# One start modulo 256 bytes for the tiles that matmuls read, and evacuations ahead of preparations in the spatial product

## The chip, the cores and the metric

One core of a Trainium2 chip runs the whole program as one launch. The metric is the device time of that launch in microseconds (us). The kernel before took 2926.91 us, the median of three runs (2926.86, 2926.91 and 2934.82).

## What is computed

Three layers in a row, all in float32, on x of 4 batches, 3072 tokens and 256 features:

```python
X = np.fft.fft(np.fft.fft(x, axis=1), axis=2).real          # layer 1
h = np.maximum(X @ w_in, 0.0)                                # layer 2
u, v = h[..., :512], h[..., 512:]
v_n = (v - mean(v)) / sqrt(var(v) + 1e-6)                    # over the 512 features
v_s = einsum("ts,bsd->btd", w_spatial, v_n) + b_spatial[None, :, None]
y = ((u * v_s) @ w_out).reshape(12288, 256)
out = (sigmoid(y @ w_gate) * (y @ w_val)) @ w_out2           # layer 3
```

`w_spatial` is 3072 by 3072: the product over tokens is most of the work.

## The kernel before, in words

Every product is done with both operands split into a high part (12 bits less, by a ScalarE cast to float32r) and a low part (VectorE subtracts the high part); `mm3` (L257) issues three matmuls for one product: high by high (L259), low by high (L260), high by low (L261). A matmul has a moving operand (up to 512 columns) and a stationary one (128 columns).

The program has three stages, one after the other on TensorE:

- **First stage** (to about 292 us): the transforms and `x @ w_in` with the transform of the features folded into it, in units per batch; tables `c1`, `c2`, `c3`, transformed rows `ph`/`pl`, weights `g`. It leaves v and u in DRAM and the mean and root of each token's v in `ln_of`.
- **Spatial stage** (to about 1824 us): the product with `w_spatial` by a Strassen-like scheme with 7 products (`ORDER`, `V_OF`, `W_OF`) of 2 batch pairs (p) and 3 column groups (c): 42 *leaves*, each of 6 steps (kp) of 24 matmuls of 512 columns into four PSUM banks. Two sets of four banks take turns.
- **Gate stage** (to the end): 144 groups of 33 matmuls, 7 products of `x` by `wg` and 4 of `g` by `wv` in each.

In the loop over leaves (from L1205) a step kp of leaf n issues, in this order: `advance(6n + kp + 3, 2)`, which on the SP queue issues the loads of two steps on (`load_due`, into the 7 buffers `st`), on ScalarE normalises the v tiles that are due (`norm_job`, L802), and for each due tile (`prepare_job`) adds two tiles on VectorE (L819 for w, L815 for v), casts the high part on ScalarE (L821), and issues the *previous* tile's low part on VectorE (L824, held back in `lows`); then the 24 matmuls; then, for kp under 4, `evacuate` of bank kp of the leaf before. A tile that is prepared in a step is read by matmuls three steps later (`LEAD = 3`), and `wr` holds four w tiles. Where c is 2, the v tiles of the next product are due as well, one each step, so that such a step prepares two tiles instead of one.

`evacuate` adds a bank into the sums on VectorE. In the 24 leaves whose product is in `FINAL` it also multiplies by u (L1062), casts the gate's high part `gh` on ScalarE (L1068), and issues the low part `gl` (L1070) only with the next evacuation, or in `finish_gate`. In steps 4 and 5 the same loop issues `second` after the step's matmuls: 12 matmuls that read all four `gh`, `gl`, a copy of the bank on ScalarE (L1109) and a store. `second` calls `finish_gate` itself. Each engine and the SP queue works strictly in the order of issue.

**Where tiles lie.** Tiles of a pool stand one behind another, each rounded up to 32 bytes in a partition; pools are stacked from the left side (from byte 16,512, which is 128 modulo 256) or from the right side (down from byte 229,344, which is 224 modulo 256). As the kernel before is laid out, the starts modulo 256 of what matmuls read are:

| stage | left side | right side |
|---|---|---|
| first | `sps`, `spc` 128; `c3` 160; `c2`, `c1` 224; `fh`, `fl` 0 | `wih`, `wil`, `fd` 128; `g`, `nts` 0; `ph`, `pl` 0 or 128; `nt` 192 |
| spatial | `vh`, `vl`, `wh`, `wl` 128 | `woh`, `wol`, `gh`, `gl` 0 |
| gate | `wg` 128; `x0` to `x6` 128 | `x7` and the four `tail` slots 0; `gh`, `gl`, `wv` 0 |

Of the kernel before, what the change touches and what calls it, by code (L numbers as in the profile page):

```python
# [9 lines left out]
F32 = mybir.dt.float32  # L10
F32R = mybir.dt.float32r
# [8 lines left out]
B, S, D = 4, 3072, 256  # L20
# [4 lines left out]
P = 128  # L25
H = 384
R3 = H + 2

ROW = 32
RP = -(-R3 // ROW) * ROW  # L30
NT_TOK = B * S

# [201 lines left out]
FINAL = {5: (0, 1), 4: (0, 0), 2: (1, 0), 6: (1, 1)}  # L234
# [3 lines left out]
def tile_kernel(ctx: ExitStack, tc: tile.TileContext, t: dict, out: bass.AP):  # L238
# [10 lines left out]
    def f(ap):  # L249
        return ap.bitcast(F32)  # L250
# [51 lines left out]
    def pool(stack, name, bufs, side="left", **kw):  # L302
        return stack.enter_context(tc.tile_pool(name=name, bufs=bufs, side=side, reuse_waits="tile", **kw))
# [1 line left out]

    r0, l0, f0 = ExitStack(), ExitStack(), ExitStack()
    lnp = pool(ctx, "lnp", 1, "right")
    ln_of = lnp.tile([P, B * 24, 2], F32, name="ln_of")
    shifts = {}
    keep = pool(r0, "keep", 1, "right")  # L310
    pqp = pool(r0, "pqp", 2, "right")
    cst = pool(l0, "cst", 1)
    xp = pool(l0, "xp", 1)
    fop = pool(l0, "fop", 3)
    fhp = pool(l0, "fhp", 3)
    ps0 = ExitStack()
# [6 lines left out]
    nts = [keep.tile([P, R3 if unit == 3 else H], F32R, name=f"nt{unit}") for unit in range(4)]  # L323
    masks = keep.tile([P, 16], F32, name="masks")[:, : 3 + B]
    sps = cst.tile([P, B + 1, 2, P], F32R, name="sps")
    spc = cst.tile([P, SP_N], F32R, name="spc")
    cc = {}

    def load_table(p, name, shapes):

        size = sum(int(np.prod(shape)) for shape in shapes.values())
        table = p.tile([P, 2 * size], F32R, name=name)
        nc.gpsimd.dma_start(table, t[name])
        for i in range(2):
            at = i * size
            for key, shape in shapes.items():
                n = int(np.prod(shape))
                ap = table[:, at : at + n]
                names = " ".join("abc"[: len(shape)])
                ap = ap.rearrange(f"p ({names}) -> p {names}", **dict(zip("abc", shape)))  # L340
                cc.setdefault(key, []).append(ap)
                at += n
# [94 lines left out]
    tmp = pool(s0, "tmp", 1, "right")  # L437
# [45 lines left out]
    xs = tmp.tile([P, B + 1, 2, P], F32, name="xs")  # L483
    nc.sync.dma_start(xs, t["xs"])

    fn = tmp.tile([P, 2 * ROW], F32, name="fn")[:, : 12 * B].rearrange("p (s k) -> p s k", s=4)
    folds(nc.gpsimd, [(0, xn, fn)])
    load_table(cst, "c3", {"c3p": (3, R3), "c3q": (3, H)})
    nc.gpsimd.dma_start(spc, t["spc"])
    fold0(2, 0)  # L490
    fold0(2, 1)
# [2 lines left out]
    rest = convert([0, 1])  # L494
# [51 lines left out]
    rest = convert([2, 3])  # L546
# [11 lines left out]

    fold0(1, 0)
    rest()  # L560
    load_table(cst, "c2", {"c2p": (3, H), "c2q": (3, H)})
    take = first_weights(0)
    sums = [fft(fold, 0, 3, q, tiles=(2, 0), end=False, early=True) for q in range(2)]
    fold0(1, 1)
# [5 lines left out]
    take()  # L570
    spread(1)
    pq = [take_fft(*sums[q], q) for q in range(2)]
    load_table(cst, "c1", {"c1": (2, 3, H)})
    mirror_samples(slice(1, B))

    def take_nyquist(ps, n, unit):
# [8 lines left out]
    stp = pool(r0, "stp", 2, "right")  # L585
# [6 lines left out]
    def own_samples(b, unit):  # L592

        nt = stp.tile([P, RP], F32R, tag="nt", name="nt", bufs=1)[:, : R3 if unit == 3 else H]
        nc.scalar.activation(nt, f(nts[unit]), AF.Identity, scale=masks[:, 3 + b : 4 + b])
        nt_of[b, unit] = nt

    def unit_blocks(pq, b, unit):
# [5 lines left out]
        nt = nt_of.pop((b, unit))  # L604
        nb = 7 if unit == 3 else 6
        tiles = {}
        stats = stp.tile([P, 7, 6], F32, name="stats")
        mv = stp.tile([P, 7, 2], F32, name="mv")
        ve, sd = (stp.tile([P, 7], F32, name=n) for n in ("ve", "sd"))
        yp = lnb[:, unit % 2, :]  # L610


# [75 lines left out]
        def ln2():  # L688

            stt = nc.vector.scalar_tensor_tensor  # L690
            nc.vector.reciprocal(yp[:, a], sd[:, a])

            stt(out=ve[:, a], in0=yp[:, a], scalar=-0.5, in1=ve[:, a], op0=ALU.mult, op1=ALU.mult)
            nc.vector.tensor_tensor(out=ve[:, a], in0=ve[:, a], in1=yp[:, a], op=ALU.mult)
            stt(out=yp[:, a], in0=ve[:, a], scalar=1.5, in1=yp[:, a], op0=ALU.add, op1=ALU.mult)
            at = b * 24 + unit * 6
            places = [(slice(0, 6), ln_of[:, at : at + 6, :])]
            if nb == 7:
                own = stp.tile([P, 1, 2], F32, name="own")
                places.append((slice(6, 7), own))  # L700
            for k, to in places:
                nc.vector.tensor_copy(to[:, :, 0], yp[:, k])
                stt(out=to[:, :, 1], in0=mv[:, k, 0], scalar=-1.0, in1=yp[:, k], op0=ALU.mult, op1=ALU.mult)  # L703
            if nb == 7:
                q = H - (R3 - P)
                queue.dma_start(ln_of[0:1, at + 3 : at + 4, :], own[q : q + 1, :, :])
# [25 lines left out]
    jobs = []  # L732
# [17 lines left out]
    jobs = full  # L750
    tail_v = [d for d in late_v if d >= 6 * len(leaves)]
    assert not tail_v
    staged, ready, lows = {}, {}, []
    state = {"load": 0, "prep": 0}

    def source(kind, key, block):
# [21 lines left out]
    def shift_of(p, i):  # L778

        first, second, sign = V_OF[i]  # L780
        if second is None:
            return columns(p, first)[:, :, 1]
        if (p, i) not in shifts:
            shifts[p, i] = lnp.tile([P, 12], F32, name=f"shift{p}{i}")
            nc.vector.tensor_tensor(
                out=shifts[p, i],
                in0=columns(p, second)[:, :, 1],
                in1=columns(p, first)[:, :, 1],
                op=ALU.add if sign > 0 else ALU.subtract,
            )  # L790
        return shifts[p, i]

    def norm_job(n):

        _, kind, key = jobs[n]
        if kind == "v":
            p, i, kp = key
            first, second, _ = V_OF[i]
            st, scale, shift = staged[n][-1], columns(p, second or first)[:, :, 0], shift_of(p, i)
            for k in range(2):  # L800
                at = slice(2 * kp + k, 2 * kp + k + 1)
                nc.scalar.activation(st[:, k, :], st[:, k, :], AF.Identity, scale=scale[:, at], bias=shift[:, at])  # L802
# [35 lines left out]
    def advance(step, loads):  # L838

        load_due(step + loads)  # L840
        due = state["prep"]
        while due < len(jobs) and jobs[due][0] <= step:
            norm_job(due)
            due += 1
        while state["prep"] < due:
            prepare_job(state["prep"])
            state["prep"] += 1

    def start_a():
        l0.close()  # L850
# [53 lines left out]
    step = 0  # L904
# [53 lines left out]
                transform(base + AT3[q], b + 1, 3, q, pqs[b + 1, 3], None)  # L958
    transform(NYQ, B, 0, 0, None, None)
    own_samples(*units[0])  # L960
    for (b, unit), follows in zip(units, units[1:] + [None]):
        blocks, later = unit_blocks(pqs[b, unit], b, unit)
        for block in blocks:
            put_off(step, block, follows if block is blocks[-1] else None)
            for do in plan.pop(step, []):
                do()
            for first, _ in ffts.get(step, []):
                first()
            for do in lns.pop(step, []):
                do()  # L970
            for _, take in ffts.get(step, []):
                take()
            step += 1
        for k, do in enumerate(later):
            lns.setdefault(step + LAG + k, []).append(do)
# [99 lines left out]
    def finish_gate(side):  # L1075
        if "low" in side:
            side.pop("low")()
# [41 lines left out]
    p, i, c = leaves[-1]  # L1119
# [73 lines left out]
    before = None  # L1193
# [9 lines left out]
    for n, leaf in enumerate(leaves[:-1]):  # L1203
        p, i, c = leaf
        base = 4 * (n % 2)  # L1205
        ps = [banks(base + d) for d in range(4)]
        side = {"g": []}
        for kp in range(6):
            advance(6 * n + kp + LEAD, 2)
            if kp == 4:  # L1210
                side_loads(leaf, side)
            wh, wl = ready["w", (p, i, c, kp)]
            vh, vl = ready["v", (p, i, kp)]
            for k in range(2):
                for d in range(4):
                    dsl = slice(d * P, d * P + P)
                    mm3(
                        ps[d],
                        (vh[:, k, dsl], vl[:, k, dsl]),
                        (wh[:, k, :], wl[:, k, :]),  # L1220
                        kp == 0 and k == 0,
                        kp == 5 and k == 1,
                    )
            if before is not None:
                if kp < 4:
                    evacuate(before[0], before[1][kp], kp, before[2])
                elif before[0][1] in FINAL:
                    second(before[0], kp - 4, 4 - base + kp - 2, before[2])
            if n and c < 2 and before[0][1] not in FINAL:
                background()  # L1230
        before = (leaf, ps, side)
# [3 lines left out]
    n, leaf = len(leaves) - 1, leaves[-1]  # L1235
# [51 lines left out]
    before = (leaf, ps, side)  # L1287
# [76 lines left out]
    for n in range(len(groups) + 2):  # L1364
# [39 lines left out]
        if now and j + 1 < len(pairs):  # L1404
            if fb == 0:
                next_steps = x_steps(j + 1, load_raw(j + 1))
            at = {3: 0, 4: 1, 5: 2, 6: 3, 7: 4, 8: 5, 9: 6, 11: 7}
# [26 lines left out]
```

## Time and profile before

| | |
|---|---|
| median of the runs | 2926.91 us |
| the profiled execution, its own time | 2935.72 us |
| its span, first to last instruction | 2933.9 us |
| TensorE busy, matmuls | 2855.7 us (97%), 12,550 matmuls |
| VectorE, ScalarE, GpSimd busy | 2023.8, 1424.8, 224.3 us |
| mean granted TensorE clock | 0.991 |

The profiled execution is nearer to the slowest of the three runs than to the other two. Matmuls overlap: one is recorded as 0.39 us long, and the next one starts about 0.23 us after it started. A busy share says little therefore; the distance from start to start (the *pitch*) and the idle times tell where TensorE's time goes.

### The profile page before, as it was taken

To read this page: it belongs to the slowest core of one execution; us is meant where nothing else is said; L and a number is where in the kernel's file an instruction comes from. 1 tells how busy PE (TensorE), PEld (TensorE's weight loads), DVE (VectorE), ACT (ScalarE), POOL (GpSimd) and SP (SyncE) were. 2 spreads that over 40 slices of the span, in tenths; PEclk is the share of its full clock that TensorE was granted. 3 is DMA by queue.
4 is the path that set the end of the run, shared out by engine and by line. 5 is a ranking of instruction groups with operands and counts; after the bars stand their busy time and mean duration, and the time that the engine had idled before them with its cause. 6 is when DMAs were issued, how large, how long until landed. Compare 5 with 4: busy or idle time off the path is not lost.

```text
span 2933.9 us, 34266 instructions
## 1 busy us (share of the span) xinstructions
PE 2855.7 (97%) x12550; PEld 2358.3 (80%) x12550; DVE 2023.8 (69%) x3001; ACT 1424.8 (49%) x2267; POOL 224.3 (8%) x333
## 2 busy tenths in 40 slices
PE   4999999999999999999999999999999999999999
PEld 4887787888877888878887878888888888888887
DVE  7777766787756567578666476866666666676665
ACT  4787444344334244334324333656555555555554
POOL 3883000111000001000000000000000000000000
PEclk9999999999999999999999999999999999999999
DMA  6877866787756677578776474200000000000000
GB/s 232 281 274 280 274 229 234 243 312 260 254 185 227 208 264 260 171 264 297 235 251 217 155 263 139 86 29 29 29 15 15 29 29 29 15 15 29 29 15 15
DMA packets 148180, 470.76 MB, mean 160 GB/s; under 512 B 16797, under 2 KB 18333, under 8 KB 147628
## 3 DMA queue, kind: packets, MB, share of 16 engines
q1 hardware_dynamic: 140540, 434.88, 43.5%
q0 software_dynamic: 4016, 21.11, 1.8%
q10 hardware_dynamic: 3456, 12.58, 1.1%
q8 instruction: 98, 1.61, 0.2%
q14 instruction: 70, 0.57, 0.1%
HBM read 385.94 MB, written 82.58 MB: 160 GB/s over the span
## 4 chain that ended last, share of the span: by engine, by line
PE 87%; DVE 6%; issue 3%; ACT 3%; DMA 1%; POOL 0%; ACTq 0%; DVEq 0%; POOLq 0%
PE bank L261 28%; PE bank L259 28%; PE bank L260 28%; DVE vl L824 1%; DVE st L815 1%; DVE g L1062 0%; PE psf L259 0%; ACT st L802 0%; DVE gl L1070 0%; DVE wl L824 0%; DMA st<-v_d 0%; PE psf L261 0%; PE psf L260 0%; DVE st L819 0%; PE psv L260 0%
## 5 line engine op out<-in xcount | busy, mean ns | idle before, releaser
L259 PE MATMUL bank<-wh,vh 128*128 128x512 f32 x2016 | 790.1, 392 | 6.0 <-DVE ln_of L703 6.0
L261 PE MATMUL bank<-wh,vl 128*128 128x512 f32 x2016 | 789.2, 391 | 0.0
L260 PE MATMUL bank<-wl,vh 128*128 128x512 f32 x2016 | 789.2, 391 | 0.0
L824 DVE TENSOR_TENSOR wl<-st,wh 128x1024 fp32r<-128x1024 f32 x252 | 311.6, 1237 | 394.9 <-ACT wh L821 394.5
L821 ACT CAST wh<-st 128x1024 fp32r<-128x1024 f32 x252 | 264.6, 1050 | 569.6 <-PE bank L261 386.5
L259 PEld LDWEIGHTS bank<-wh,vh 128*128 128x128 f32 x2016 | 381.5, 189 | 85.9 <-DVE ln_of L703 6.7
L260 PEld LDWEIGHTS bank<-wl,vh 128*128 128x128 f32 x2016 | 382.0, 189 | 80.1
L261 PEld LDWEIGHTS bank<-wh,vl 128*128 128x128 f32 x2016 | 381.4, 189 | 80.1
L1317 DVE TENSOR_TENSOR t<-t,bank 128x512 f32<-128x512 f32 x144 | 98.9, 687 | 247.7 <-PE bank L261 247.7
L259 PE MATMUL bank<-x,wgh 128*128 128x512 f32 x673 | 265.1, 394 | 0.4 <-ACT t L1329 0.4
L261 PE MATMUL bank<-x,wgl 128*128 128x512 f32 x673 | 264.2, 393 | 0.0
L260 PE MATMUL bank<-x,wgh 128*128 128x512 f32 x673 | 264.2, 393 | 0.0
L1338 DVE TENSOR_TENSOR gl<-s,gh 128x512 fp32r<-128x512 f32 x288 | 199.3, 692 | 57.7 <-ACT gh L1336 44.5
L259 PE MATMUL bank<-gh,wv 128*128 128x512 f32 x576 | 226.2, 393 | 0.8 <-ACT gh L1331 0.8
L261 PE MATMUL bank<-gh,wv 128*128 128x512 f32 x576 | 226.6, 393 | 0.0
L260 PE MATMUL bank<-gl,wv 128*128 128x512 f32 x576 | 225.5, 391 | 0.2 <-DVE gl L1338 0.2
L819 DVE TENSOR_TENSOR st<-st 128x1024 f32<-128x1024 f32 x180 | 219.5, 1220 | 5.9 <-DMA st<-in_wt 5.7
L1308 ACT ACTIVATE s<-s 128x512 f32<-128x512 f32 x144 | 91.0, 632 | 149.9 <-DVE s L1307 149.9
L1109 ACT COPY x<-bank 128x512 f32<-128x512 f32 x48 | 28.3, 589 | 258.9 <-PE bank L261 255.9
L259 PEld LDWEIGHTS bank<-x,wgh 128*128 128x128 f32 x673 | 126.4, 188 | 30.4 <-ACT t L1329 0.9
L260 PEld LDWEIGHTS bank<-x,wgh 128*128 128x128 f32 x673 | 127.0, 189 | 28.8
L261 PEld LDWEIGHTS bank<-x,wgl 128*128 128x128 f32 x673 | 126.3, 188 | 28.6
(237 smaller groups left out, 4586.1 us busy)
## 6 DMA issues: line engine op xcount, KB each, us to landing
st<-in_wt SPq DMA_DIRECT2D x432, 512.0 KB, 5.2
st<-v_d SPq DMA_DIRECT2D x144, 512.0 KB, 4.8
u<-u_d SPq DMA_DIRECT2D x96, 256.0 KB, 4.0
u_d<-tu SPq DMA_DIRECT2D x48, 384.0 KB, 3.8
v_d<-tv SPq DMA_DIRECT2D x69, 256.0 KB, 4.3
xt<-in_xh SPq DMA_DIRECT2D x24, 512.0 KB, 4.2
x_d<-x ACTq DMA_DIRECT2D x24, 512.0 KB, 2.9
raw<-x_d SPq DMA_DIRECT2D x24, 512.0 KB, 4.2
```

Source lines behind the costliest of these rows:

```text
L259: nc.tensor.matmul(out=ps, lhsT=w[0], rhs=x[0], start=first, stop=False, **kw)
L260: nc.tensor.matmul(out=ps, lhsT=w[0], rhs=x[1], start=False, stop=False, **kw)
L261: nc.tensor.matmul(out=ps, lhsT=w[1], rhs=x[0], start=False, stop=last, **kw)
L815: nc.vector.scalar_tensor_tensor(out=st, in0=st, scalar=scale[:, at], in1=tiles[1][:, k, :], op0=ALU.mult, op1=op)
L819: nc.vector.tensor_tensor(out=tiles[0], in0=tiles[0], in1=tiles[1], op=op)
L821: nc.scalar.copy(hl[0], tiles[0])
L824: lows.append(lambda: nc.vector.tensor_tensor(out=hl[1], in0=tiles[0], in1=f(hl[0]), op=ALU.subtract))
L1109: nc.scalar.copy(side["x2"][:, o, :], ps)
L1308: nc.scalar.activation(s1, s1, AF.Sigmoid)
L1317: nc.vector.tensor_tensor(out=g["t2"], in0=g["t2"], in1=g["b"], op=ALU.add)
L1338: nc.vector.tensor_tensor(out=l, in0=s, in1=f(h), op=ALU.subtract)
```

## The change

Three things are changed.

1. **Places.** `ROW` is 64 in place of 32, so that `ph`, `pl` and `nt` are 1,792 bytes wide instead of 1,664. `ln_of` and the shifts become slices of one tile of 1,280 bytes, where `lnp` had 1,408. Small tiles (`stats`, `mv`, `ve`, `sd`, `own`) become slices of one tile `small`; three tiles called `rest` are only padding; the tables `c1`, `c2`, `c3` are allocated ahead of `spc`.
2. **Order in a spatial step.** `evacuate` (kp under 4) or `finish_gate` (kp 4 and 5) of the leaf before is issued ahead of `advance`. `second` stays behind the matmuls.
3. **Normalisation.** A v tile with kp = 0 is normalised on ScalarE in the step before the one that prepares it (set `normed` keeps it from being done twice).

```diff
-ROW = 32
+ROW = 64
...
-    ln_of = lnp.tile([P, B * 24, 2], F32, name="ln_of")
+    ln_all = lnp.tile([P, 320], F32, name="ln_all")
+    ln_of = ln_all[:, : B * 48].rearrange("p (k two) -> p k two", two=2)
...
     xp = pool(l0, "xp", 1)
+    xp.tile([P, 32], F32, name="rest")
...
     sps = cst.tile([P, B + 1, 2, P], F32R, name="sps")
+    tables = {name: cst.tile([P, t[name].shape[1]], F32R, name=name) for name in ("c1", "c2", "c3")}
     spc = cst.tile([P, SP_N], F32R, name="spc")
...
+    tmp.tile([P, 32], F32, name="rest")
+    fn = tmp.tile([P, 64], F32, name="fn")[:, : 12 * B].rearrange("p (s k) -> p s k", s=4)
...
-        stats = stp.tile([P, 7, 6], F32, name="stats")
-        mv = stp.tile([P, 7, 2], F32, name="mv")
-        ve, sd = (stp.tile([P, 7], F32, name=n) for n in ("ve", "sd"))
+        small = stp.tile([P, 72], F32, name="small")
+        stats = small[:, 0:42].rearrange("p (i k) -> p i k", k=6)
+        mv = small[:, 42:56].rearrange("p (i k) -> p i k", k=2)
+        ve, sd = small[:, 56:63], small[:, 63:70]
...
-            shifts[p, i] = lnp.tile([P, 12], F32, name=f"shift{p}{i}")
+            at = B * 48 + 12 * len(shifts)
+            shifts[p, i] = ln_all[:, at : at + 12]
...
-        if kind == "v":
+        if kind == "v" and n not in normed:
+            normed.add(n)
...
         while state["prep"] < due:
             prepare_job(state["prep"])
             state["prep"] += 1
+        while due < len(jobs) and jobs[due][0] == step + 1:
+            if jobs[due][2][-1] == 0 and due in staged:
+                norm_job(due)
+            due += 1
...
+    stp.tile([P, 48], F32, name="rest", bufs=1)
...
         for kp in range(6):
+            if before is not None:
+                if kp < 4:
+                    evacuate(before[0], before[1][kp], kp, before[2])
+                else:
+                    finish_gate(before[2])
             advance(6 * n + kp + LEAD, 2)
...
             if before is not None:
-                if kp < 4:
-                    evacuate(before[0], before[1][kp], kp, before[2])
-                elif before[0][1] in FINAL:
+                if kp >= 4 and before[0][1] in FINAL:
                     second(before[0], kp - 4, 4 - base + kp - 2, before[2])
```

## Rows read from the trace of the kernel before

**Rows 1.** The page, parts 1 and 4: busy time by engine; chain by engine.
```profile
PE 2855.7 (97%) x12550; PEld 2358.3 (80%) x12550; DVE 2023.8 (69%) x3001; ACT 1424.8 (49%) x2267; POOL 224.3 (8%) x333
...
PE 87%; DVE 6%; issue 3%; ACT 3%; DMA 1%; POOL 0%; ACTq 0%; DVEq 0%; POOLq 0%
```

**Rows 2.** Windows of PE: stretch, length us, busy (matmuls), clock, DMA share, GB/s.
```profile
1280.00:1570.00 290.00, 290.00 (x1280) 1.00 0.75 251
1850.00:2390.00 540.00, 540.00 (x2344) 1.00 0.09 30
2390.00:2920.00 530.00, 530.00 (x2294) 1.00 0.05 19
```

**Rows 3.** PE in order of time, spatial stage: start us, length us, operation.
```profile
999.95 0.39 PE L259 MATMUL bank<-wh,vh 128*128 128x512 f32 x1
...
1010.60 0.40 PE L261 MATMUL bank<-wh,vl 128*128 128x512 f32 x1
1010.84 0.39 PE L259 MATMUL bank<-gh,woh 128*128 128x512 f32 x1
...
1013.33 0.40 PE L261 MATMUL bank<-gh,wol 128*128 128x512 f32 x1
```

**Rows 4.** PE in order of time, gate stage, one group of 33 matmuls.
```profile
2299.22 0.40 PE L259 MATMUL bank<-x,wgh 128*128 128x512 f32 x1
...
2306.86 0.40 PE L259 MATMUL bank<-x,wgh 128*128 128x512 f32 x1
```

**Rows 5.** Waits of PE, whole span: total us, times, longest us.
```profile
PE bank L260 <- DVE gl L1070: 15.1, 6, 3.3
```

**Rows 6.** PE in order of time at one such wait (last: idle before).
```profile
499.25 0.39 PE L259 MATMUL bank<-gh,woh 128*128 128x512 f32 x1
502.00 0.50 PE L260 MATMUL bank<-gl,woh 128*128 128x512 f32 x1 [2.37 <-DVE gl L1070]
...
503.53 0.63 PE L259 MATMUL bank<-wh,vh 128*128 128x512 f32 x1
503.95 0.63 PE L260 MATMUL bank<-wl,vh 128*128 128x512 f32 x1
...
506.45 0.39 PE L260 MATMUL bank<-wl,vh 128*128 128x512 f32 x1
```

**Rows 7.** Window there: us, PE, PEld, DVE, ACT, POOL, clock, DMA.
```profile
504.00:512.00 8.00, 8.00 (x32) 6.53 (x31) 6.41 (x9) 3.41 (x4) 0.00 (x0) 0.85 1.01 389
```

**Rows 8.** DVE in order of time, steps 2 to 4 of that leaf.
```profile
485.86 1.22 DVE L824 TENSOR_TENSOR wl<-st,wh 128x1024 fp32r<-128x1024 f32 x1
...
493.00 1.21 DVE L824 TENSOR_TENSOR wl<-st,wh 128x1024 fp32r<-128x1024 f32 x1
...
496.53 1.22 DVE L819 TENSOR_TENSOR st<-st 128x1024 f32<-128x1024 f32 x1
...
501.26 0.68 DVE L1070 TENSOR_TENSOR gl<-g,gh 128x512 fp32r<-128x512 f32 x1
```

**Rows 9.** DVE in order of time, at the start of that leaf.
```profile
472.06 1.46 DVE L815 SCALAR_TENSOR_TENSOR st<-st,ln_of 128x512 f32<-128x512 f32 x2 [7.25 <-ACT st L802]
```

**Rows 10.** ACT in order of time: first normalisation, last gh.
```profile
471.21 1.52 ACT L802 ACTIVATE st<-st,shift,ln_of 128x512 f32<-128x512 f32 x2 [0.42 <-ACT x L1109]
...
496.04 0.62 ACT L1068 CAST gh<-g 128x512 fp32r<-128x512 f32 x1 [1.88 <-DVE g L1062]
```

**Rows 11.** Waits of ACT, whole span, and of the SP queue, 330 to 1750.
```profile
ACT wh L821 <- PE bank L261: 386.5, 110, 4.4
...
ACT st L802 <- DMA st<-v_d: 36.3, 23, 4.0
...
SPq L1081 <- DVE g L1062: 223.0, 45, 18.8
```

**Rows 12.** PE in order of time, first stage.
```profile
160.76 0.34 PE L259 MATMUL psu<-ph,gh 128*128 128x384 f32 x1
...
162.54 0.40 PE L259 MATMUL psv<-gh,ph 128*128 128x512 f32 x1
```

More of the change, by code (lines that the diff above doesn't have):

```diff
@@ L325, in tile_kernel, with load_table @@
     sps = cst.tile([P, B + 1, 2, P], F32R, name="sps")
+    tables = {name: cst.tile([P, t[name].shape[1]], F32R, name=name) for name in ("c1", "c2", "c3")}
     spc = cst.tile([P, SP_N], F32R, name="spc")
     cc = {}
-    def load_table(p, name, shapes):
+    def load_table(name, shapes):
         size = sum(int(np.prod(shape)) for shape in shapes.values())
-        table = p.tile([P, 2 * size], F32R, name=name)
+        table = tables[name]
         nc.gpsimd.dma_start(table, t[name])
@@ L484, in tile_kernel @@
     nc.sync.dma_start(xs, t["xs"])
-    fn = tmp.tile([P, 2 * ROW], F32, name="fn")[:, : 12 * B].rearrange("p (s k) -> p s k", s=4)
+    tmp.tile([P, 32], F32, name="rest")
+    fn = tmp.tile([P, 64], F32, name="fn")[:, : 12 * B].rearrange("p (s k) -> p s k", s=4)
     folds(nc.gpsimd, [(0, xn, fn)])
-    load_table(cst, "c3", {"c3p": (3, R3), "c3q": (3, H)})
+    load_table("c3", {"c3p": (3, R3), "c3q": (3, H)})
     nc.gpsimd.dma_start(spc, t["spc"])
@@ L560, in tile_kernel @@
     rest()
-    load_table(cst, "c2", {"c2p": (3, H), "c2q": (3, H)})
+    load_table("c2", {"c2p": (3, H), "c2q": (3, H)})
     take = first_weights(0)
@@ L572, in tile_kernel @@
     pq = [take_fft(*sums[q], q) for q in range(2)]
-    load_table(cst, "c1", {"c1": (2, 3, H)})
+    load_table("c1", {"c1": (2, 3, H)})
     mirror_samples(slice(1, B))
@@ L698, in ln2 @@
             if nb == 7:
-                own = stp.tile([P, 1, 2], F32, name="own")
+                own = small[:, 70:72].rearrange("p (i k) -> p i k", k=2)
                 places.append((slice(6, 7), own))
@@ L752, in tile_kernel @@
     assert not tail_v
-    staged, ready, lows = {}, {}, []
+    staged, ready, lows, normed = {}, {}, [], set()
     state = {"load": 0, "prep": 0}
```

## The prediction

> **What bounds the kernel now.** I read the page first: TensorE is busy 97% of the span and carries 87% of the chain [rows 1]. A busy share can't show whether matmuls run as fast as they could, so the next view is the windows of TensorE, in which I divide length by count. A window also counts the 1.7 matmuls that are under way at its edge (0.39 us long, one starting every 0.23 us), so 1.7 comes off each count. That gives 290.00/1278.3 = 226.9 ns in a stretch of the spatial stage, but 540.00/2342.3 = 230.5 and 530.00/2292.3 = 231.2 ns in the gate stage, at the same full clock and with no idle time in any of the three [rows 2]. The starts say it finer: in the spatial stage 47 matmuls from 999.95 to 1010.60 take 226.6 ns each [rows 3]; a group of 33 in the gate stage takes 7.64 us, 231.5 ns each [rows 4]. All have 512 columns, the same type and the same three forms, so something that is not work costs 4 to 5 ns a matmul in the gate stage.
>
> The second loss is waiting. Leaving the start of the program and the first leaf aside, TensorE's list of waits has one entry of weight: the second matmul form of a `second` waits for `gl`, 6 times, 15.1 us [rows 5]. Each is followed by a dear stretch [rows 6]: after the wait the pitch is 0.42 to 0.43 us instead of 0.227, the 1.2 GHz level in place of 2.4, and the window there shows a granted clock of 0.85 [rows 7].
>
> **Part 1, the places.** From the sizes in the code: `lnp` shrinks from 1,408 to 1,280 bytes, so that everything on the right side moves up by 128 bytes; `keep`, `cp` and `gp` then start at 128 modulo 256, where the left side starts already. `ph`, `pl` and `nt` of 1,792 bytes are 7 times 256; `nt`, `rest` and the two `small` fill 2,560 bytes, 10 times 256; the tables behind `sps` start at 128, and `spc`, `xp` and its padding bring `fh` and `fl` to 128 (18,496 + 6,176 + 128 + 32 leave no remainder). So in the spatial and the gate stage all operands start at 128, and in the first stage all but slices of `c3` and `spc` and the last windows of `ph`.
>
> What is it worth? In the spatial stage `wh` and `vh` are both at 128, and `gh` and `wo` both at 0. Both kinds run at the low pitch: 226.6 ns from 999.95 on, and 11 matmuls from 1010.84 to 1013.33 at 226.4 ns [rows 3]. Only where the class changes is a start late: 1010.60 to 1010.84 is 0.24 us for what should be 0.227 [rows 3]; at this resolution 0.01 to 0.02 us for each change of class. In the gate stage the class changes inside every group (`x` and `wg` at 128, `x7` and `tail` at 0, `gh` and `wv` at 0), and moving and stationary operand differ in part of the products. With one class everywhere it should run as the spatial stage does: (230.5 - 226.7) x 2342 = 9.0 us and (231.2 - 226.7) x 2292 = 10.4 us, together **19.5 us**. Bounds: 0, if pitch doesn't hang on places, and 21 us with the 120 matmuls outside these windows. I take 19.5, since both classes alone show the lower pitch.
> In the spatial stage 46 `second` have two changes each: 92 x 0.01 to 0.02 = 0.9 to 1.8 us; I take **1.0**. In the first stage 10 matmuls of 384 columns take 1.78 us, 178 ns [rows 12], where 226.7 less 128 columns at 2.4 GHz would be 173.4; at 4.6 ns for each of 1,086 matmuls from 60 us on that is 5.0 us at most. TensorE waits for ScalarE and VectorE there too, which takes part of it back, so between 0 and 5; I take **1.5**. The padding, the merged small tiles and the tables' new places add no instruction. What VectorE writes into the merged tiles it writes in its own order, so I cost them at nothing; bounds are nothing and a wait of the 0.2 us kind in 16 units, 3 us.
>
> One rule speaks against this part. The Trainium skill, SBUF — State Buffer, section "Who interferes with whom", gives TensorE two independent read ports and says "PE and ACT never wait on anyone"; the section "Operand start alignment" asks an operand only to start at a multiple of its element size, and adds that this is about legality, not speed. By that, part 1 would be worth 0 instead of 22 us, which is the first rival below. The trace does not agree fully: 226.6 and 231.5 ns stand side by side at one clock.
>
> **Part 2, evacuation first.** At the wait in rows 6 VectorE is not idle but late. One step of preparing two tiles and evacuating a bank takes it 493.00 - 485.86 = 7.14 us [rows 8], while TensorE's 24 matmuls take 24 x 0.2267 = 5.44 us. This happens where c is 2 and both this leaf and the one before are followed by a `second`, six times. `gl` is issued behind the preparation of step 4, which runs from 496.53 to 501.26 [rows 8], while its input `gh` is done at 496.04 + 0.62 = 496.66 [rows 10]. Moved ahead of that preparation, `gl` starts at 496.7 instead of 501.26 and ends at 497.4. TensorE asks for it at 499.25 + 0.23 = 499.48 [rows 6]: 2.1 us to spare even with nothing else moved. More is moved: the evacuation of bank 3 itself goes ahead of step 3's preparation. So all six waits should go.
> What one costs: from 499.25 to 506.45 there are 13 pitches, 7.20 us in place of 13 x 0.2267 = 2.95, so 4.25 us, of which 2.37 is the listed wait and 1.88 the clock and the way back to it [rows 6]. Six times: 15.1 + 6 x 1.88 = **26.4 us**. Bounds: 15.1 if the clock fell anyway, 26.4 if it doesn't.
>
> What moves behind: each preparation now stands behind up to four VectorE operations of 0.68 us (2.7 us). Who waits for it? TensorE, three steps later. The spare time follows from the code and one row: ScalarE's cast of a w tile waits for TensorE 110 times, 386.5 us [rows 11], because the fourth w buffer is free only when TensorE has left the step before; so in most steps a tile is ready one cast (1.05 us) and one subtraction (1.24 us) after that, 3 x 5.44 - 2.3 = 14 us before it is read. 14 covers 2.7. Behind the moved evacuation on ScalarE stands the cast `gh`, on the SP queue the load of u; both come earlier than before, and loads of two steps on come later by the same 2.7 us. What is late next in these leaves is VectorE itself: 6 preparations of 4.7 us and 4 evacuations of 2.4 us are 38 us, against TensorE's 32.6 for the products and 5.4 for the two `second`, 38 us: just even, with 14 us of lead ahead of it.
>
> **Part 3, normalising ahead.** At the start of such a leaf VectorE stood 7.25 us [rows 9], because the first normalisation stood on ScalarE behind the bank copy of `second` (it began at 471.21, straight after it) [rows 10]. Issued in the step before, it runs ahead of that copy. This gives VectorE up to 7 us in each of 13 products; none of it is on TensorE's path by itself, so **0 us**, but it adds to the 2.1 us to spare. Queued behind the normalisation on ScalarE are the bank copy and the next `gh`. It can wait for its load, as it does 23 times now, up to 4.0 us [rows 11]; 13 x 4.0 = 52 us of ScalarE, half idle, under 14 us of lead: 0 on the path.
>
> **The sum.** 19.5 + 1.0 + 1.5 + 26.4 = 48.4 us. The profiled span of 2933.9 becomes 2885.5, and its own time of 2935.72 becomes 2887.3. The profiled execution lies 8.8 us above the median and 0.9 above the slowest of the three runs. Nothing in the sum hangs on that difference, so I take it off the median: 2926.91 - 48.4 = **2878.5 us**; with runs like the profiled one it is 2887.
>
> **Rivals.**
> *Places don't matter.* The gate stage keeps 231 ns, for a reason that only goes along with the stage (more semaphores, the change of banks). For: the spatial stage is the only witness of the lower pitch. Against: both classes there have it, and changes of class cost there too. Time 2926.91 - 26.4 = 2900.5. Chance 0.11.
> *The waits stay in another place.* VectorE needs 38 us for 38, so a late load or a cast in these leaves puts `gl` late again, or another operand. For: 7.14 against 5.44 us. Against: the 2.1 us and the 7.25 us. Time 2926.91 - 22.0 = 2904.9. Chance 0.09.
> *Neither does anything.* 2926.9. Chance 0.03.
> *Preparations come too late, and the kernel is slower.* SP waits 223.0 us for u buffers already, up to 18.8 us [rows 11], and that load now stands ahead of a step's w and v loads, which follow the evacuation instead of leading it. If the loads slip by more than the 14 us of lead, TensorE runs at VectorE's pace in the 7 leaves that both evacuate a gated product and prepare v: 4 steps x (7.14 - 5.44 + 1.9 for the clock) = 14.4 us in each, 101 us in all: 2878.5 + 101 = 2979.5. It decides from 14 us of slip on, that is five evacuations in a row. Chance 0.04.
>
> **How the numbers follow.** My forecast has 0.73. 0.3%, about what a measurement can tell from no change, is 8.8 us: faster takes the forecast and the first two rivals, 0.93; same 0.03; slower 0.04. The range runs from 2868 (5 us in the first stage, 21 in the gate stage, and some 5 for a clock that falls less often elsewhere) to 2902, which takes in 2887 for runs like the profiled one and the first rival.
>
> **What would show it.** Right: no wait for `gl` in TensorE's list; gate groups of 33 x 226.7 = 7.48 us; spatial stage 27 us shorter. Step by step: if gate pitch stays at 231, part 1 is wrong; if it lies between, the classes explain only part; if waits for `wl` or `vl` appear, the lead was overrated; if `gl` is waited for still, VectorE's pace was. The forecast fails as a whole if loads or a clock that falls in new places eat the gain.

## The result, and the profile after

The changed kernel takes **2888.65 us**, the median of four runs (2888.45 to 2888.82). Four runs of the kernel before, the three that were known and one beside it, have a median of 2930.34 us; the ratio is 0.9857, with a 95% interval of 0.9839 to 0.9875. The profiled execution took 2888.82 us, with a span of 2886.7 us.

Where the time went is told by the starts of the stages, read from the order of time of TensorE (first matmul to first matmul of the next stage; the gate stage to the start of its last one):

| us | before | after | difference |
|---|---|---|---|
| first stage | 273.9 | 274.1 | +0.3 |
| spatial stage | 1533.1 | 1505.2 | -27.9 |
| gate stage | 1105.0 | 1085.7 | -19.3 |
| span | 2933.9 | 2886.7 | -47.2 |

The rest of 0.3 us lies ahead of the first matmul and behind the last.

The page of the changed kernel, busy time and chain by engine:

```profile
PE 2823.3 (98%) x12550; PEld 2349.2 (81%) x12550; DVE 2018.2 (70%) x3001; ACT 1426.1 (49%) x2267; POOL 212.1 (7%) x333
...
PE 91%; POOL 3%; DVE 2%; ACT 1%; issue 1%; DMA 1%; ACTq 0%; SPq 0%; POOLq 0%; DVEq 0%
```

TensorE has more of the chain than in [rows 1], 91% against 87%. GpSimd has 3% of it, where [rows 1] had 0%; the first stage, further down, comes back to that.

TensorE's windows in the same views as [rows 2] (stretch, length, busy with the number of matmuls, granted clock, DMA share, GB/s):

```profile
1280.00:1570.00 290.00, 290.00 (x1281) 1.00 0.74 251
1824.00:2364.00 540.00, 539.92 (x2382) 1.00 0.09 30
2364.00:2870.00 506.00, 506.00 (x2234) 1.00 0.05 19
```

In the gate stage 540 us now hold 2,382 matmuls where [rows 2] had 2,344. With 1.7 taken off for the edges that is 226.9 ns each, and 506.00/2232.3 = 226.7 in the next window: the pitch of the spatial stage. One group of 33, to be set beside [rows 4]:

```profile
2299.01 0.39 PE L259 MATMUL bank<-x,wgh 128*128 128x512 f32 x1
...
2306.49 0.39 PE L259 MATMUL bank<-x,wgh 128*128 128x512 f32 x1
```

7.48 us, as against 7.64.

TensorE's list of waits, the five longest (total us, times, longest):

```profile
PE psg L259 <- ACT wih L463: 28.6, 2, 17.5
PE psv L628 <- ACT nt L599: 7.9, 6, 2.0
PE psg L260 <- DVE wil L468: 6.2, 2, 3.1
PE bank L259 <- DVE ln_all L708: 5.7, 1, 5.7
PE psf L259 <- DVE pl L435: 5.2, 7, 1.4
```

The entry of [rows 5], `gl`, is gone and no other has come in its place; what stands here was there before. At the place of [rows 6] TensorE now runs through the `second` without a break:

```profile
498.67 0.39 PE L259 MATMUL bank<-gh,woh 128*128 128x512 f32 x1
498.89 0.39 PE L260 MATMUL bank<-gl,woh 128*128 128x512 f32 x1
499.12 0.39 PE L261 MATMUL bank<-gh,wol 128*128 128x512 f32 x1
```

VectorE at the same leaf, beside [rows 8] and [rows 9]:

```profile
464.87 0.69 DVE L1057 TENSOR_TENSOR g<-c,bank 128x512 f32<-128x512 f32 x1 [9.13 <-PE bank L261]
...
485.52 0.68 DVE L1057 TENSOR_TENSOR g<-c,bank 128x512 f32<-128x512 f32 x1
...
486.72 0.68 DVE L1074 SCALAR_TENSOR_TENSOR g<-u,g 128x512 f32<-128x512 f32 x1
...
491.52 1.22 DVE L831 TENSOR_TENSOR wl<-st,wh 128x1024 fp32r<-128x1024 f32 x1
492.65 0.68 DVE L1082 TENSOR_TENSOR gl<-g,gh 128x512 fp32r<-128x512 f32 x1
493.26 1.22 DVE L826 TENSOR_TENSOR st<-st 128x1024 f32<-128x1024 f32 x1
```

The evacuation of bank 0 begins at 464.87, as soon as TensorE is done with the bank. It waited 9.13 us for that: a new wait, in front of VectorE, and harmless. The last `gl` runs from 492.65 to 493.33, ahead of the preparation (493.26), and TensorE reads it at 498.89: 5.6 us to spare. On ScalarE the leaf's first normalisation, beside [rows 10], now stands ahead of the bank copy instead of behind it:

```profile
462.90 1.52 ACT L809 ACTIVATE st<-st,ln_all 128x512 f32<-128x512 f32 x2
469.63 0.59 ACT L1121 COPY x<-bank 128x512 f32<-128x512 f32 x1 [5.21 <-PE bank L261]
```

### The profile page after: what moved, and what is told of

It reads as the page before. It is cut to its first block, busy times and chain, and to the rows that moved or that the text cites. A ratio compares the mean times of both kernels' runs of the same rounds, so it can differ in the third digit from the quotient of the medians.

```text
span 2886.7 us, 34266 instructions
## 1 busy us (share of the span) xinstructions
PE 2823.3 (98%) x12550; PEld 2349.2 (81%) x12550; DVE 2018.2 (70%) x3001; ACT 1426.1 (49%) x2267; POOL 212.1 (7%) x333
## 4 chain that ended last, share of the span: by engine, by line
PE 91%; POOL 3%; DVE 2%; ACT 1%; issue 1%; DMA 1%; ACTq 0%; SPq 0%; POOLq 0%; DVEq 0%
PE bank L259 30%; PE bank L260 30%; PE bank L261 30%; POOL et L377 0%; POOL xt L378 0%; DMA xt<-in_xh 0%; POOL fo L362 0%; POOL xt L360 0%; PE psf L259 0%; DMA u_d<-tu 0%; PE psv L260 0%; PE psv L259 0%; PE psv L261 0%; PE psu L261 0%; PE psu L260 0%
## 5 line engine op out<-in xcount | busy, mean ns | idle before, releaser
L831 DVE TENSOR_TENSOR wl<-st,wh 128x1024 fp32r<-128x1024 f32 x252 | 309.7, 1229 | 235.5 <-ACT wh L828 230.6
L809 ACT ACTIVATE st<-st,ln_all 128x512 f32<-128x512 f32 x168 | 127.6, 808 | 66.3 <-DMA st<-v_d 52.4
```

The lines of the kernel that those rows point to most:

```text
L831: lows.append(lambda: nc.vector.tensor_tensor(out=hl[1], in0=tiles[0], in1=f(hl[0]), op=ALU.subtract))
```

## The experiments

Two theories are to be told apart for each half of the gain. For the gate stage: a matmul runs at 226.7 ns where all operands start at one place modulo 256 bytes; or the pitch belongs to something else. For the spatial stage: `gl` is late because it is issued behind a preparation; or VectorE is late as a whole. And a third question came up with the runs: why the kernel before spreads over more than 8 us, and the changed one over 0.4.

### The places alone, and the parts of the order one by one

All four kernels keep the new places. In the first, the old order stands and nothing is normalised ahead:

```diff
-            if before is not None:
-                if kp < 4:
-                    evacuate(before[0], before[1][kp], kp, before[2])
-                else:
-                    finish_gate(before[2])
             advance(6 * n + kp + LEAD, 2)
...
-                if kp >= 4 and before[0][1] in FINAL:
+                if kp < 4:
+                    evacuate(before[0], before[1][kp], kp, before[2])
+                elif before[0][1] in FINAL:
...
-        while due < len(jobs) and jobs[due][0] == step + 1:
-            ...
```

> The changed kernel with the old order of a spatial step and without the earlier normalisation: only the places are changed. Theory: the spatial stage keeps its six waits (15.1 us, 26 us with the clock) and is about 1489 us from its first matmul to the gate stage's first, after 1532 to 1533 less nothing else than 1 us for the changes of class; the gate stage takes 1085.7 us, as in the changed kernel; span about 2913 us. Rival (places alone do nothing): span 2933.

Measured: 2912.09 us, the median of four runs (2911.68 to 2912.77); ratio to the kernel before 0.9930, interval 0.9915 to 0.9945; span 2911.0. The gate stage takes 1085.7 us, as in the changed kernel to a tenth. TensorE's waits in the spatial stage:

```profile
PE bank L260 <- DVE gl L1078: 14.6, 6, 2.7
PE bank L259 <- DVE ln_all L708: 5.9, 1, 5.9
```

The six waits are all there. (The 1489 us of the expectation are those from the second leaf to the gate stage, first matmul to first matmul; 1487.8 were measured.) So the places give the whole of the gate stage's gain and none of the spatial stage's, apart from about 1 us of changes of class.

The second kernel has the old order too, but keeps the earlier normalisation (the last hunk above is not undone).

> Places and the earlier normalisation, with the old order of evacuation. Theory: VectorE starts the six leaves up to 7 us earlier, which is more than the 2.5 us by which gl was late; so the waits for gl go or shrink although gl is still behind the preparation of step 4: span 2887 to 2895 us. Rival (only the order counts): the six waits stay, 15 us, span about 2913.

Measured: 2897.3 us in one run, span 2895.5.

```profile
PE bank L260 <- DVE gl L1082: 5.9, 6, 1.3
PE bank L259 <- DVE ln_all L708: 5.7, 1, 5.7
```

Six waits again, but 5.9 us in place of 14.6, and the clock did not fall behind any of them. Both expectations are half right, and the span is 0.5 us above the range of the theory. Each wait is 1.45 us shorter on the mean, and none has gone. At the first of the six leaves, counted from the first matmul of the second leaf (333.29 us with the places alone, 334.02 here), the addition to the v tile comes 7.3 us earlier (464.76 here, 471.35 there). But VectorE then stands 6.13 us for the cast of the next w tile, whose low part comes only 1.4 us earlier, and by as much the wait is shorter (0.96 in place of 2.38).

The third kernel has the evacuation first, and only the normalisation is put back (only the last hunk is undone).

> Places and the evacuation first, without the earlier normalisation. Theory: no wait for gl, span 2886 to 2888 us, since gl has 2.1 us to spare with the order alone. Rival: without the earlier normalisation some of the six waits stay, 2 us or more each.

Measured: 2887.1 us in one run, span 2885.3. No `gl`:

```profile
PE bank L259 <- DVE ln_all L708: 6.8, 1, 6.8
PE psu L259 <- ACT eu L668: 0.5, 1, 0.5
PE bank L259 <- ACT t L1340: 0.4, 1, 0.4
```

The stretch from the second leaf to the gate stage takes 1463.36 us both here and in the changed kernel. **The earlier normalisation adds nothing**, once the evacuation is first.

The fourth kernel takes the least that should do. Only `finish_gate` goes ahead of the preparations of steps 4 and 5, that is one VectorE operation in a leaf (in step 5 nothing is left for it to issue), and the evacuations stay behind them:

```diff
-            if before is not None:
-                if kp < 4:
-                    evacuate(before[0], before[1][kp], kp, before[2])
-                else:
-                    finish_gate(before[2])
+            if before is not None and kp >= 4:
+                finish_gate(before[2])
             advance(6 * n + kp + LEAD, 2)
```

> Places, and of the new order only this: in steps 4 and 5 finish_gate is issued ahead of the preparations; the evacuations stay behind them, and there is no earlier normalisation. Theory: the wait for gl at the places-only kernel is 2.4 us each, and gl is held up by the preparation of step 4 (4.7 us), so moving gl alone takes all six waits away: no wait for gl, spatial stage 1463 us, span about 2886. Rival (gl is held up because the evacuations as a whole come late, so that its input gh is late too): waits of 0.5 us or more stay.

Measured: 2888.1 us in one run, span 2886.3, and 1463.36 us from the second leaf to the gate stage.

```profile
PE bank L259 <- DVE ln_all L708: 5.7, 1, 5.7
PE psu L259 <- ACT eu L668: 0.5, 1, 0.5
PE bank L259 <- ACT t L1339: 0.4, 1, 0.4
```

So what held TensorE up was the place of one operation of 0.68 us in the queue, behind 4.7 us of preparation for a step that comes three steps later. The rival falls: the evacuations may stay late.

### How far apart two places must be

Four kernels are the changed one with more padding behind the tiles of the spatial and the gate stage: 32 more elements for 128 bytes, as below, and 16, 8 and 64 for 64, 32 and 256. This moves all tiles of the right side (`wo`, `gh`, `gl`, `x7`, `tail`, `wv`) down by that much, while the left side (`v`, `w`, `wg`, `x0` to `x6`) stays at 128. The starts are worked out from the sizes in the code; the traces hold no addresses.

```diff
-    cp.tile([P, 24], F32, name="rest")
+    cp.tile([P, 24 + 32], F32, name="rest")
```

> The changed kernel with 128 bytes more of padding on the right side behind the tiles of the spatial and the gate stage: woh, wol, gh, gl, x7, tail and wv start at 0 modulo 256 again, the left side stays at 128. Theory (one class modulo 256): gate stage 1105 us instead of 1085.7, pitch 230.8 instead of 226.7 ns; spatial stage 1 us longer at the 92 changes of class. Rival (the gain of the gate stage came from another part of the change): 1086 us.

> The same with 64 bytes: right side at 64, left side at 128 modulo 256. Theory (any difference modulo 256 costs the same): gate stage about 1105 us. Rival A (the cost grows with the distance): about 1095. Rival B (only the place modulo 64 counts): 1086.

> The same with 32 bytes: right side at 96, left side at 128 modulo 256. Theory: about 1105 us in the gate stage. Rival A (grows with the distance): about 1090. Rival B (only the place modulo 64 or more, rounded down, or modulo 32 counts): 1086 in the second case.

> The same with 256 bytes: both sides at 128 modulo 256, but the right side at 384 and the left at 128 modulo 512. Theory (modulo 256 is all that counts): gate stage 1085.7 us, pitch 226.7 ns. Rival (the first stage, whose tiles are at one place modulo 256 after the change but at two modulo 512, still has a pitch of 230.9 ns for 512 columns, so it is modulo 512): about 1105 us.

TensorE's windows of the gate stage, in this order: 128, 64, 32 and 256 bytes.

```profile
1824.00:2364.00 540.00, 540.00 (x2343) 1.00 0.09 31
2364.00:2870.00 506.00, 506.00 (x2189) 1.00 0.05 19
```

```profile
1824.00:2364.00 540.00, 540.00 (x2339) 1.00 0.08 30
2364.00:2870.00 506.00, 506.00 (x2189) 1.00 0.06 20
```

```profile
1824.00:2364.00 540.00, 540.00 (x2340) 1.00 0.08 30
2364.00:2870.00 506.00, 506.00 (x2196) 1.00 0.06 20
```

```profile
1824.00:2364.00 540.00, 539.93 (x2382) 1.00 0.08 30
2364.00:2870.00 506.00, 506.00 (x2234) 1.00 0.05 19
```

| right side moved by | gate stage, us | pitch there, ns | spatial stage from leaf 1, above 226.7 ns, us | span, us |
|---|---|---|---|---|
| 0 (the changed kernel) | 1085.7 | 226.7 | 0.0 | 2886.7 |
| 32 bytes | 1104.4 | 230.7 | 3.1 | 2908.0 |
| 64 bytes | 1106.5 | 231.1 | 2.5 | 2908.3 |
| 128 bytes | 1105.0 | 230.8 | 0.9 | 2906.6 |
| 256 bytes | 1085.7 | 226.7 | 0.0 | 2886.4 |

The pitch is the mean over the gate stage of starts less than 25 ns late; the fourth column sums what the same starts lie above 226.7 ns.

With 128 bytes, the classes of the kernel before are back, and so is its gate stage to the tenth: 1105.0 us. With 32 bytes the loss is the same, so the cost in the gate stage does not grow with the distance. And 256 bytes cost nothing, although the two sides then differ modulo 512. The theory stands in each of the four, for 512 columns and these two stages. Each is one run, on another chip than the kernels of the last section; the run with 256 bytes repeats the changed kernel's gate stage there, and five profiles of the kernel before have 1104.9 to 1105.0 us in it. The padding also moves tiles that only VectorE and ScalarE touch, but their place alone costs nothing: in the kernel before they stood at 0 in the spatial stage while most matmuls read at 128, at 226.6 ns [rows 3].

In the spatial stage, where the class only changes at the 46 `second`, the price of a change is larger the smaller the step is: 0.9, 2.5 and 3.1 us over 92 changes, or 10, 27 and 33 ns each. It is not paid in one pitch. On the mean over the 46 `second`, the pitch into the first `gh` by `wo` matmul and the next one are 232.3 and 230.9 ns at 128 bytes, and the ones behind are back at 226.7; at 32 bytes six pitches in a row are raised there.

In the gate stage the kinds of product change every three to twelve matmuls, and there the pitch is raised all through, not only where moving and stationary operand differ. Six matmuls of `gh` by `wv`, all at 0, in the kernel before:

```profile
2301.30 0.40 PE L259 MATMUL bank<-gh,wv 128*128 128x512 f32 x1
...
2302.69 0.39 PE L259 MATMUL bank<-x,wgh 128*128 128x512 f32 x1
```

1.39 us, 231.7 ns each; on the mean over 285 such stretches the four pitches in the middle lie between 228.6 and 229.6 ns. 11 matmuls of `gh` by `wo`, at 0 as well, ran at 226.4 in the spatial stage [rows 3]. So one place has to hold for the whole run of matmuls, not for each matmul by itself. Why the pitch does not come back to 226.7 inside such a stretch is open.

### Why the kernel before spreads

Its 32 runs beside and in these experiments lie between 2926.5 and 2935.0 us, with a median of 2932.8. Four of them were profiled:

> The kernel before, once more, to see where its two levels of time (2926.9 and 2934) part. Theory: the six waits for gl with 4.2 us each are in every run, and the levels differ by how long the clock is low after the start of the program or of the spatial stage (in the first trace the clock was low for 13.65 us around the start of that stage). Then a run at the lower level has a span near 2925 us and a granted clock higher by about 2 x 8 / 2930 = 0.005 than the 0.991 of the first trace. Rival: the lower level has fewer waits, and then its clock differs by less than that, with the idle time missing.

> The kernel before, one more look. Theory for its spread of 2926.5 to 2935 us: the six waits for gl (14 to 15 us) are in every execution, and what differs is after how many of them the clock falls for 3.4 us, at 1.7 us each. So the time is about 2933.0 plus or minus 1 with six low stretches, 2931 with five, 2928 with three or four, 2926.5 with two or three, while the sum of the waits differs by less than 1.5 us. Rival: the number of low stretches doesn't go with the time; the start of the program or of the spatial stage makes the difference.

> The kernel before, another look, with the same expectations: 1.7 us of time for each stretch of low clock behind a wait for gl (theory), or no such relation (rival).

> The kernel before, a third look, with the same expectations: 1.7 us of time for each stretch of low clock behind a wait for gl (theory), or no such relation (rival).

| profile | time, us | waits for `gl` (times, us) | low clock behind them (times) | stalls in the spatial stage from leaf 1, us |
|---|---|---|---|---|
| the one of the prediction | 2935.7 | 6, 15.1 | 6 | 26.3 |
| `before_look1` | 2933.7 | 6, 14.2 | 6 | 25.3 |
| `before_look2` | 2932.8 | 6, 14.2 | 5 | 23.8 |
| `before_again` | 2932.4 | 6, 14.1 | 5 | 23.8 |
| `before_look3` | 2932.2 | 6, 15.4 | 4 | 23.1 |

(The last column sums the pitches that lie 25 ns or more over 226.7.) Windows of 25 us around the first, fifth and sixth wait, in `before_look1` and then in `before_look3`:

```profile
495.00:520.00 25.00, 22.64 (x93) 0.93 0.95 322
...
1574.00:1599.00 25.00, 22.70 (x93) 0.93 0.64 218
1693.00:1718.00 25.00, 22.61 (x93) 0.93 0.94 321
```

```profile
495.00:520.00 25.00, 22.64 (x93) 0.93 0.92 317
...
1574.00:1599.00 25.00, 22.70 (x101) 1.00 0.69 234
1693.00:1718.00 25.00, 22.60 (x100) 1.00 0.96 346
```

A granted clock of 0.93 in a window of 25 us is one stretch of 3.4 us at the 1.2 GHz level. In `before_look1` it follows all six waits, in `before_look3` the first four. Where it follows, the windows shown hold 93 matmuls, elsewhere 100 or 101. (The fourth wait, not shown, was the longest of `before_look3`, 3.4 us.) So the waits are in every execution that was profiled, and the clock behind them is not: each fall costs 1.5 us (25.3 against 23.8, with the same waits) to 1.9 us (23.8 against 23.1, with 1.2 us more of waits in the second). The order of the five times is that of the falls, but the times lie closer together than was expected: 2932.8 and 2932.4 with five falls, not 2931, and 2932.2 with four, not 2928.

The theory of `before_again`, that the levels part at the start of the program or of the spatial stage, has fallen: the clock was low at these two places for 30.7 us in `before_again` and for 23.9 us in `before_look1`, which was the slower one.

What is open: the lowest times, 2926.5 to 2926.9, were seen in three of 32 runs and in no profile. At 1.5 to 1.9 us a fall they would need two falls or fewer behind the six waits, and that was not seen. What is on record points that way. Of 28 runs the mean granted clock is known. It is 0.991 or 0.992 in 17 of the 18 runs from 2931.9 us up (0.993 in `before_look3`), 0.993 in all nine from 2929.5 to 2930.7, and 0.995 in the one of 2926.5; in the changed kernel, which has no such wait, it is 0.994 to 0.996. One fall is 0.0006 of this mean, but the mean does not tell where the clock was low.

## Why the prediction was right, and where it was not

- **Gate stage, 19.5 us: right.** Measured 19.3, and the kernel with 128 bytes of padding gives it back. The step that it rested on, that both classes alone show the low pitch in the spatial stage, is confirmed from the other side: all operands at 128, then 256 bytes apart, and the pitch is 226.7 in both. The rule of the Trainium skill that spoke against it (SBUF — State Buffer, "Who interferes with whom") does not decide the case: it tells which engines wait for one another, and here 19.3 us hang on start addresses alone. The sentence of the Trainium skill in that page's section "Operand start alignment", that element alignment is a matter of legality and not of speed, leaves room for that. The two causes that the prediction names, changes of class inside a group and products whose two operands differ, were not told apart; a stretch of the gate stage that is all at 0, between two changes, was dear too.
- **Changes of class, 1.0 us: right.** 1.1 us were there, and none is left. That smaller steps cost more at a change was not foreseen.
- **Six waits with their clock, 26.4 us: right.** 26.3 us of stalls in the profiled execution, 0.0 after. The mechanism was right down to the one operation, as the run with only `finish_gate` shows. `gl` was to end at 497.4 with nothing else moved; it ended at 493.3, since more was. By the condition that the prediction gives there would be seven such leaves in the loop, as in its last rival, not six: the seventh evacuates product 6, which has one VectorE operation less for each bank, and prepares a v that needs no addition.
- **What moves behind: right.** No wait for `wl` or `vl` appeared. The SP queue waits for u buffers 229.8 us in the same stretch, 46 times and up to 22.6 us, a little more than in [rows 11], and nothing came of it.
- **Normalisation ahead, 0 us on the path: right**, by 1463.36 us with and without it. But of the "up to 7 us" that it was to give VectorE, 1.4 us were left one w tile later at the first of the six leaves.
- **First stage, 1.5 us: wrong.** It got 0.3 us longer in the two profiles compared. Over all profiles it takes 273.9 to 274.5 us in the five of the kernel before and 273.5 to 274.4 in the nine with the new places, 0.3 us less on the mean: a gain of 1.5 us was not there. The 10 matmuls of [rows 12] did get faster, 1.73 us in place of 1.78, which is 173 ns each and the low pitch for 384 columns:

```profile
160.36 0.34 PE L259 MATMUL psu<-ph,gh 128*128 128x384 f32 x1
...
162.09 0.39 PE L259 MATMUL psv<-gh,ph 128*128 128x512 f32 x1
...
163.71 0.34 PE L259 MATMUL psu<-ph,gh 128*128 128x384 f32 x1
```

But the 7 matmuls of 512 columns behind them take 1.62 us, 231 ns, with every operand at 128 modulo 256 by the sizes in the code. In the kernel before they took as much, from the 162.54 of [rows 12] to here:

```profile
164.16 0.34 PE L259 MATMUL psu<-ph,gh 128*128 128x384 f32 x1
```

So the step that failed is the price, 4.6 ns for each of 1,086 matmuls, read from one row of ten. From 60 us on, without late starts and stretches of low clock, the pitch of 384 columns was 175.1 ns on the mean and fell to 174.4, and that of 512 columns was 230.6 and is 231.0: 0.7 ns for some 640 matmuls, or 0.5 us, were to be had. The upper bound of 5 us was wrong with it. GpSimd's share of the chain explains nothing: it was 2% in `before_look1`, with the old places, and is 0% in the run with 128 bytes, with the new ones:

```profile
PE 86%; DVE 6%; POOL 2%; issue 2%; ACT 2%; DMA 1%; ACTq 0%; DVEq 0%; SPq 0%; POOLq 0%
```

```profile
PE 95%; DVE 2%; ACT 1%; issue 1%; DMA 1%; POOL 0%; ACTq 0%; DVEq 0%; POOLq 0%
```

Why the pitch of 512 columns stays at 231 there is open: in this stage one place modulo 256 was not enough. Modulo 512, which the run with 256 bytes excludes for the gate stage, is no explanation; what is different in this stage is that 3 or 4 matmuls of 512 columns stand between some of 384 and 386. This was not tried.

- **The sum, 48.4 us: right to 1.2 us** in the profiled execution (47.2 in the span; 2888.8 against 2887.3 in its own time).
- **The time, 2878.5 us: 10.2 us too low, within the range.** The step that failed is the last one of the sum: "Nothing in the sum hangs on that difference, so I take it off the median". 8.8 of the 10.2 us are that difference, and the other 1.4 are the miss of the sum, the first stage above all. The 26.4 us held the price of clocks that fell behind all six waits in the profiled execution, 26.3 - 15.1 = 11.2 us, and the executions differ in how many of these fell, as far as five of them were profiled. I took a loss that the slow end of the spread has from a time at the fast end; two of the three runs known then were at 2926.9, and in all only three of 32 are below 2929. Made against the profiled execution's own time, the forecast was 2887.3, and 2888.8 was measured. That the runs at 2926.9 had few of these falls is likely and was not seen. The range held because it was drawn to take in 2887. The changed kernel has no such wait left behind which the clock could fall, and its runs lie within 0.4 us.

The rivals: *places don't matter*, *neither does anything* and *preparations come too late* have fallen. Of *the waits stay in another place* one half is seen: with the earlier normalisation alone they stay, at 5.9 us.

## What to carry to other kernels

Where matmuls stand back to back, compare their pitch between stages before believing a busy share; if it differs at one clock and one shape, look at where the operands start modulo 256 bytes, and pad pools until all have one place; in the first stage this was not enough. An operation that TensorE waits for belongs ahead of preparations for later steps in the queue of its engine: moving one subtraction took 24 us off the kernel with the places alone (1487.8 to 1463.4 us from the second leaf to the gate stage). And take a sum from the execution in which its terms were read, above all where a term is a clock that may or may not fall.

## What was not expected of the hardware

In a steady run a matmul of 512 columns in these types starts every 226.7 ns, and every 230.7 to 231.1 ns on the mean in the gate stage, where products at two places that are 32, 64 or 128 bytes apart modulo 256 follow one another every few matmuls; 256 bytes apart cost nothing. There the cost is not higher at a larger distance. A single change between two places, in the spatial stage, costs more at 32 bytes (33 ns, spread over six pitches or more) than at 128 (10 ns, over two). In the first stage 512 columns stay at 231 ns with one place. Waits of 2.3 to 2.4 us were sometimes followed by 3.4 us at 1.2 GHz and sometimes not, at the same place of the same program; the waits of 0.8 to 1.3 us in the run with the earlier normalisation alone were not.
